# A chunked recurrence with the two heads of a pair on partition halves, transposed G and H, and the inverse applied inside the step

## The chip, the cores and the metric

One core of a Trainium2 chip runs the program; the others are idle. Its engines are TensorE (PE; its weight loads are listed apart as PEld), VectorE (DVE), ScalarE (ACT), GpSimd (POOL) and the sync engine SP, which only starts DMAs. The metric is the device time of one execution in microseconds (us); less is better.

## The reference

Two parts. First a linear recurrence on a 40 by 40 state, for 4 batches x 8 heads and 768 time steps; then a two-layer network on its outputs, 3072 rows of 320.

```python
for t in range(S):                       # S = 768, D = 40, float32
    y[:, :, t] = einsum('bhd,bhde->bhe', r_t, state)
    Sa = einsum('bhde,bhe->bhd', state, a_t)
    state = state * w_t[..., None, :] - einsum('bhd,bhe->bhde', Sa, b_t) \
            + einsum('bhd,bhe->bhde', v_t, k_t)
x = y.transpose(0, 2, 1, 3).reshape(3072, 320)
h = x @ w_in                             # 320 x 2048
out = (h * tanh(softplus(h))) @ w_out    # 2048 x 320
```

## The kernel before

**Chunks.** Time is cut into 12 chunks (`nch`) of 64 steps (`C`). Inside a chunk the recurrence becomes matrix products. With w's running products P and their inverses E folded into a and into b and k, the vectors u that the state is corrected by obey a triangular system: u = -(1 - G)^-1 (a S + H v), where G holds the products of a with b and H those of a with k, both strictly triangular in time. The outputs and the next state are then products of r, b, k, v, u and the old state S.

**Indices.** The 32 batch-head pairs are split as 2 x 2 x 8: `be` and `al` are one bit each and `s` runs over 8. Before, the partition halves of the inputs hold `al` (0 to 39 and 64 to 103), and `be` is a loop.

**Preparation of a chunk**, `pre_a(c, be)`, twice a chunk. SP loads w, a, b and k. VectorE reduces, scans forward to P (which is also stored for later, `pD`) and backward to E, multiplies a by P (L152) and b, k by E (L170). ScalarE spreads a block-diagonally into `ad` (L155). For each s one matmul of the full array gives G, H and the transposed a at once (L186, 128x168 out); ScalarE and VectorE copy the pieces into `gp`, the 32-blocks of G, and `ha`, which holds H under a mask and a (L188 to L193). Transposes give `bkn`, time on partitions (L202). Small matmuls turn w's products into `RW` (L166).

**The inverse of two chunks**, `pre_inv(n)` and `post_inv`. VectorE transposes 32-blocks (L209), solves 128 triangular 32-systems by 30 rounds of a multiply and an add (L214, L216), and transposes back (L218, L220). Two rounds of 32-square matmuls (L232, L241) give the lower left block of the 64-inverse, ScalarE lays it out block-diagonally in `bdT` (L249 to L251), and one matmul for each s (L258) multiplies the inverse into `ha`: `KT`, copied by L260.

**The step of a chunk**, `step(c)`, for two groups `g` of 8 pairs each, in the order of `SORD`. `step_a`: VS holds v and the state; 16 matmuls of VS with KT give u transposed at once (L286), which L288 writes into UVT beside v. `step_b`: UVT times r (L320), masked by VectorE into UVQ (L322). `step_u`: u itself by a transpose and a matmul with the identity for each s (L294, L296). `step_d`: the state transposed (L310). `step_c`: outputs and state update (L340, L345), then L348 to L352. `step_loads` starts the next chunk's loads from GpSimd's queue, and L376 stores the chunk's output.

**The network**, class `Mlp`. Weights arrive as 64-bit floats and are converted piece by piece (`load_f32`, `split`: L465 to L501), each split in two float32r parts. `early` loads a quarter of w_in, `first` the rest once the preparation's pools are free (`pctx`), `second` (at the last pair of chunks) the first `NO1` = 3 of 8 pieces of w_out, `third` the others when the recurrence's pools are free. `mlp1` (L591) and `mlp2` (L611 to L613) are TensorE work on 256 rows at a time, mlp2 running `LAG` = 3 quarters behind.

**Order.** A planner places every instruction on its engine's queue, in program order unless `tc.high_priority(offset)` moves a block forward (or back, if negative). The program order is preparation and inverse for pair 0, preparation for pair 1, then for each pair n the letters of `ORDER`: `0` and `1` are its two steps, `i` the inverse of pair n+1, `a` the preparation of pair n+2, `A` the call of `first`. The table `OFF` holds the offsets by block. Queues run in order; a waiting instruction holds up all that is behind it on its engine.

Of the kernel before, what the change touches and what calls it, by code (L numbers as in the profile page):

```python
# [7 lines left out]
F32 = mybir.dt.float32  # L8
F32R = mybir.dt.float32r
AF = mybir.ActivationFunctionType  # L10
ALU = mybir.AluOpType
# [4 lines left out]
NHA = 8  # L16
# [3 lines left out]
NKT = 2  # L20
# [10 lines left out]
NAD = 2  # L31
# [16 lines left out]
def layouts(inp, S=768):  # L48
    nch = S // C

    def v(x):
        return x[:, :, :S].reshape(4, 2, 2, 2, nch, C, 40)

    r, k, vv, w, a, b = (v(inp[n]) for n in 'rkvwab')
    o = {}
    wt = w.transpose(4, 2, 1, 6, 3, 0, 5).reshape(nch, 2, 2, 40, 8, C)
    wa = np.zeros(wt.shape[:4] + (1040,), np.float32)
    wa[..., :520].reshape(wt.shape[:4] + (8, 65))[..., 1:] = wt
    wa[..., 528:] = a.transpose(4, 2, 1, 6, 3, 0, 5).reshape(nch, 2, 2, 40, 512)
    o['wa'] = wa  # L60
    bt, kt = (x.transpose(4, 2, 1, 6, 3, 0, 5).reshape(nch, 2, 2, 40, 8, 1, C) for x in (b, k))
    bk = np.concatenate([bt, kt], -2)
    bk[:, 1] = np.concatenate([kt, bt], -2)[:, 1]
    o['bk'] = bk.reshape(nch, 2, 2, 40, 8, 128)
    o['rD'] = np.ascontiguousarray(r.transpose(4, 1, 6, 2, 3, 0, 5)).reshape(nch, 2, 40, 16, C)
    o['vD'] = np.ascontiguousarray(vv.transpose(4, 1, 6, 3, 0, 2, 5)).reshape(nch, 2, 40, 8, 128)
    o['vN'] = np.ascontiguousarray(vv.transpose(4, 2, 5, 3, 0, 1, 6)).reshape(nch, 2, C, 16, 40)
    p = np.arange(128)
    cst = np.zeros((128, 328), np.float32)
    cst[:, :128] = np.eye(128)  # L70
    cst[:, 128:192] = (p[:, None] % 64) < np.arange(64)
    cst[:, 192:256] = np.arange(64) < (p[:, None] // 64) * 32 + p[:, None] % 32
    cst[:, 256:296] = (p[:, None] % 64) == np.arange(40)
    cst[:, 296:328] = np.arange(32) < p[:, None] % 32
    o['cst'] = cst
    return o


def attention(ctx, tc, I, yD, pD, nch, M):
# [11 lines left out]
    ci = pool("ci", 1, ictx)  # L91
# [4 lines left out]
    cst = cs.tile([128, 328], F32, name="cst")  # L96
    ident = cst[:, 0:128]
    maskQ = cst[:, 128:192]
    maskH = cst[:, 192:256]
    maskG = cst[:, 296:328]  # L100
    wab = [cp.tile([128, 1040], F32, name=f"wa{i}") for i in range(NWA)]
    bkb = [cp.tile([128, 8, 168], F32, name=f"bk{i}") for i in range(NWA)]
    adb = [cp.tile([128, 8, 2, 2, 32], F32, name=f"ad{i}") for i in range(NAD)] * (2 // NAD)
    d1 = cp.tile([128, 584], F32, name="d1")
    bdT = [ci.tile([128, 8, 2, 64], F32, name=f"bdT{i}") for i in range(2)]
    z = cs.tile([128, 1], F32, name="z")
    V.memset(z, 0.0)
    for w, b in zip(wab, bkb):
        V.memset(w, 1.0)
        G.memset(b, 0.0)  # L110
    for t in [d1] + [x.rearrange("p s k a t -> p (s k a t)") for x in adb[:NAD]]:
        A.copy(t, z.broadcast_to(t.shape))
    for t in bdT:
        G.memset(t, 0.0)
    VS = [cs.tile([128, 2, 344], F32, name=f"VS{be}") for be in range(2)]
    UVT = cs.tile([128, 8, 256], F32, name="UVT")
    UVQ = [cs.tile([128, 16, 104], F32, name=f"UVQ{be}") for be in range(2)]
    bdr = [cs.tile([128, 2, 8, 2, 64], F32, name=f"bdr{i}") for i in range(NBR)] * (2 // NBR)
    ST = [cs.tile([128, 8, 64], F32, name=f"ST{g}") for g in range(2)]
    for t in VS + [UVT] + bdr[:NBR] + ST:  # L120
        G.memset(t, 0.0)

    RW, W2, HA, BKN, GP, KT = {}, {}, {}, {}, {}, {}
    LQ, SQ, OQ, PQ = (dict(S=SP, G=G, A=A)[x] for x in QS)

    def pre_a(c, be):
        n = 2 * c + be
        wa, bk, ad = wab[n % NWA], bkb[n % NWA], adb[n % 2]
        for al in range(2):
            q = slice(al * 64, al * 64 + 40)  # L130
            LQ.dma_start(out=wa[q], in_=I['wa'][c, be, al])
        for al in range(2):
            q = slice(al * 64, al * 64 + 40)
            LQ.dma_start(out=bk[q, :, 0:128], in_=I['bk'][c, be, al])
        if (c, be) == (0, 0):
            LQ.dma_start(out=cst, in_=I['cst'])
            for t in bkb:
                A.copy(t[:, :, 128:168], cst[:, 256:296].unsqueeze(1).broadcast_to([128, 8, 40]))
        wz, a = wa[:, 0:521], wa[:, 528:1040]
        P = pw.tile([128, 520], F32, name="P", bufs=NP)  # L140
        E = wa[:, 520:1040]
        w2 = pw.tile([128, 2, 8], F32, name="w2", bufs=4)
# [8 lines left out]
        a3 = a.rearrange("p (s t) -> p s t", t=64)  # L151
        V.tensor_tensor(out=a3, in0=a3, in1=P3[:, :, 0:64], op=ALU.mult)  # L152
        for al in range(2):
            q = slice(al * 64, al * 64 + 64)
            A.copy(ad[q, :, :, al], a[q].rearrange("p (s k t) -> p s k t", k=2, t=32))  # L155
# [3 lines left out]
        W2[be] = w2  # L159
        if be == 1:  # L160

            RW[c] = wk.tile([128, 2, 16], F32, name="rw", bufs=4)
            pt = ps_g.tile([128, 2, 16], F32, name="pa")
            for b2 in range(2):
                for al in range(2):
                    PE.matmul(pt[b2 * 64:b2 * 64 + 64, al], ident[:, al * 64:al * 64 + 64], W2[b2].rearrange("p a b -> p (a b)"),  # L166
                              start=(al == 0), stop=True, skip_group_check=True)
            A.copy(RW[c], pt)
        bk4 = bk[:, :, 0:128].rearrange("p s (x t) -> p s x t", x=2)
        V.tensor_tensor(out=bk4, in0=bk4, in1=E3[:, :, 0:64].unsqueeze(2).broadcast_to([128, 8, 2, 64]), op=ALU.mult)  # L170
        for al in range(2):
            PQ.dma_start(out=pD[c, be, :, al], in_=P[al * 64:al * 64 + 40])

        if c % 2 == 0 and be == 0:
            GP[c // 2] = iw.tile([128, 32, 2, 32], F32, name="GP", bufs=NGP)
        gp = GP[c // 2]
        u0 = (c % 2) * 16 + be * 8
        ha = iw.tile([128, 8, 104], F32, name="HA", bufs=NHA)
        HA[c, be] = ha
        oa, oh = (0, 40) if be == 0 else (64, 0)  # L180
        og, ok = (0, 64) if be == 0 else (64, 0)
        for s0 in (0, 3, 6):
            m = min(3, 8 - s0)
            pt = ps_g.tile([128, 3, 168], F32, name="pa")
            for j in range(m):
                PE.matmul(pt[:, j], ad[:, s0 + j].rearrange("p k a t -> p (k a t)"), bk[:, s0 + j], start=(j == 0), stop=True,  # L186
                          skip_group_check=True)
            A.mul(gp[0:64, u0 + s0:u0 + s0 + m, 1], pt[0:64, 0:m, og:og + 32], -1.0)  # L188
            A.mul(gp[64:128, u0 + s0:u0 + s0 + m].rearrange("p u k i -> p u (k i)"), pt[64:128, 0:m, og:og + 64], -1.0)
            A.copy(ha[:, s0:s0 + m, oa:oa + 40], pt[:, 0:m, 128:168])  # L190
            V.tensor_tensor(out=ha[:, s0:s0 + m, oh:oh + 64], in0=pt[:, 0:m, ok:ok + 64],
                            in1=maskH.unsqueeze(1).broadcast_to([128, m, 64]), op=ALU.mult)
        V.tensor_tensor(out=gp[:, u0:u0 + 8, 1], in0=gp[:, u0:u0 + 8, 1], in1=maskG.unsqueeze(1).broadcast_to([128, 8, 32]),  # L193
                        op=ALU.mult)

        bkn = wk.tile([128, 664], F32, name="bkn", bufs=NBKN)
        BKN[c, be] = bkn
        G.memset(bkn[:, 640:664], 0.0)
        for s0 in (0, 4):
            pt = ps_g.tile([128, 4, 2, 64], F32, name="pa")  # L200
            for j in range(4):
                PE.transpose(pt[:, j].rearrange("p a b -> p (a b)"), bk[:, s0 + j, 0:128], ident)  # L202
            A.copy(bkn[:, s0 * 80:s0 * 80 + 320].rearrange("p (s a e) -> p s a e", a=2, e=40), pt[:, :, :, 0:40])

    def pre_inv(n):
# [3 lines left out]
        V.transpose(X.rearrange("p t j -> p j t"), gp[:, :, 1].rearrange("p u j -> p j u"))  # L209
# [7 lines left out]
        TT = iw.tile([128, 32, 32], F32, name="TT", bufs=NTT)  # L217
        V.transpose(TT.rearrange("p u t -> p t u"), X)  # L218
        T1 = gp[0:64, :, 0]
        V.transpose(T1, TT[0:64])  # L220
        return TT, T1

    def post_inv(n, TT, T1):
        gp = GP[n]
        for h in range(2):
            with at(tc, 'T%d' % h):
                px = ps_a.tile([64, 16, 32], F32, name="pa")
                for j in range(16):
                    u = h * 16 + j
                    for al in range(2):  # L230
                        q = slice(64 + al * 32, 96 + al * 32)
                        PE.matmul(px[al * 32:al * 32 + 32, j], gp[q, u, 0], TT[q, u], start=(j == 0), stop=True,  # L232
                                  skip_group_check=True)
                X = iw.tile([64, 16, 32], F32, name="X2", bufs=NX2)
                A.copy(X, px)
# [430 lines left out]
```

## Time and profile before

| | |
|---|---|
| time of the runs | 859.57 us median of 3 (859.17 to 859.66) |
| the profiled execution | 858.42 us, of which the span of instructions is 856.6 us |
| busy: PE, PEld, DVE, ACT, POOL | 769.2, 695.8, 466.2, 429.8, 123.5 us |
| granted TensorE clock, mean | 0.95 |
| last chunk's output stored | from 510 us |

The profile page gives busy time of each engine and, in rows of 40 digits, the busy tenths of each slice of 21.4 us. "By stage" is a table of busy time in chosen stretches. A timeline row gives start, length, engine, source line, operation, tiles written and read, shape and count. A group's row gives count, busy time, mean length in ns, and the idle time of the engine before its instructions with what ended most of it. An f32 matmul appears as two records.

### The profile page before, as it was taken

The page shows a single profiled execution, that of the slowest core. Times are in us where ns is not written, and L with a number is a line of the kernel's source. Part 1 is how long each engine was busy: PE and PEld are TensorE (multiplying, and loading weights), DVE is VectorE, ACT ScalarE, POOL GpSimd, SP SyncE. Part 2 cuts the span into 40 slices and gives each one's busy share as a digit, 9 for nine tenths or more (in the row PEclk, how much of TensorE's full clock was granted, in tenths as well). Part 3 has the DMA queues.
Part 4 walks back from the last instruction along what each step waited for, and adds up shares of the span by engine and source line. Part 5 has one row for each costly group of instructions (what it writes and reads, how often), then busy time and mean ns, then how long its engine had stood idle before and what let it go on. Part 6 is the DMA issues. An engine that isn't in the chain of part 4 may idle for free.

```text
span 856.6 us, 19033 instructions
## 1 busy us (share of the span) xinstructions
PE 769.2 (90%) x7904; PEld 695.8 (81%) x7904; DVE 466.2 (54%) x975; ACT 429.8 (50%) x937; POOL 123.5 (14%) x206
## 2 busy tenths in 40 slices
PE   2545899899999999998798989999999999999998
PEld 2434777777778777876776889999999999999998
DVE  6789869758758856878663728422221222222110
ACT  4533647674564686557557626433333333333331
POOL 8100022233123213321212200000000000000000
PEclk9855699999979999999899999999999999999999
DMA  5622224443232334423425746201211121100000
GB/s 165 156 70 62 84 56 90 97 115 92 68 103 80 96 86 110 102 64 101 117 81 130 187 97 184 60 18 36 53 39 30 38 54 34 34 20 17 16 1 31
DMA packets 59750, 65.87 MB, mean 77 GB/s; under 512 B 25920, under 2 KB 49472, under 8 KB 59664
## 3 DMA queue, kind: packets, MB, share of 16 engines
q1 hardware_dynamic: 49296, 40.94, 17.2%
q0 software_dynamic: 10368, 23.72, 11.7%
q8 instruction: 62, 1.02, 0.5%
q14 instruction: 24, 0.20, 0.1%
HBM read 52.72 MB, written 11.86 MB: 75 GB/s over the span
## 4 chain that ended last, share of the span: by engine, by line
PE 59%; ACT 9%; DVE 3%; DMA 3%; issue 1%; SPq 0%; DVEq 0%; ACTq 0%
PE ph L591 19%; PE po L611 6%; PE po L612 6%; PE po L613 6%; PE pq L320 3%; PE pa L258 3%; PE pu L296 3%; PE pq L340 2%; PE pa L186 2%; PE pu L294 2%; PE pu L286 2%; PE pq L345 2%; DMA cv_d<-in_wo 2%; PE pu L310 1%; PE pa L202 1%
## 5 line engine op out<-in xcount | busy, mean ns | idle before, releaser
L591 PE MATMUL ph<-xh,w_ih 128*128 128x256 f32 x576 | 148.8, 284 | 0.0
L593 ACT ACTIVATE g<-ph 128x512 f32<-128x512 f32 x96 | 57.1, 597 | 179.0 <-PE ph L591 178.8
L597 DVE TENSOR_TENSOR gl<-g,gh 128x1024 fp32r<-128x1024 f32 x48 | 58.6, 1225 | 160.1 <-ACT gh L596 159.8
L186 PE MATMUL pa<-bk,ad 128*128 128x168 f32 x384 | 86.0, 374 | 46.5 <-DVE bk L170 16.7
L591 PE MATMUL ph<-xh,w_il 128*128 128x256 f32 x576 | 124.0, 283 | 0.0
L611 PE MATMUL po<-w_oh,gh 128*128 128x320 f32 x384 | 118.1, 310 | 1.5 <-ACT w_oh L500 1.5
L612 PE MATMUL po<-w_ol,gh 128*128 128x320 f32 x384 | 118.7, 309 | 0.0
L613 PE MATMUL po<-w_oh,gl 128*128 128x320 f32 x384 | 118.4, 309 | 0.0
L186 PEld LDWEIGHTS pa<-bk,ad 128*128 128x128 f32 x384 | 70.4, 232 | 52.9 <-issue 25.7
L591 PEld LDWEIGHTS ph<-xh,w_ih 128*128 128x128 f32 x576 | 109.5, 190 | 0.2 <-issue 0.2
L591 PE MATMUL ph<-xl,w_ih 128*128 128x256 f32 x384 | 100.6, 284 | 0.0
L591 PEld LDWEIGHTS ph<-xh,w_il 128*128 128x128 f32 x576 | 96.5, 191 | 0.2 <-issue 0.2
L611 PEld LDWEIGHTS po<-w_oh,gh 128*128 128x128 f32 x384 | 71.9, 188 | 2.2 <-ACT w_oh L500 2.2
L591 PEld LDWEIGHTS ph<-xl,w_ih 128*128 128x128 f32 x384 | 73.2, 191 | 0.1
L612 PEld LDWEIGHTS po<-w_ol,gh 128*128 128x128 f32 x384 | 72.2, 188 | 0.1
L613 PEld LDWEIGHTS po<-w_oh,gl 128*128 128x128 f32 x384 | 72.2, 188 | 0.0
L258 PE MATMUL pa<-bdT,HA 128*104 128x128 f32 x384 | 54.1, 294 | 10.4 <-ACT bdT L251 8.2
L216 DVE TENSOR_TENSOR XL<-XL,tmp 128x30 f32<-128x30 f32 (+9 forms) x180 | 59.0, 328 | 2.6
L214 DVE TENSOR_TENSOR tmp<-XL 128x30 f32<-128x30 f32 (+9 forms) x180 | 58.4, 324 | 2.5
L258 PEld LDWEIGHTS pa<-bdT,HA 128*104 128x104 f32 x384 | 47.5, 182 | 14.8 <-ACT bdT L251 9.5
L320 PE MATMUL pq<-bdr,UVT 128*128 128x128 f32 x384 | 51.1, 284 | 2.8 <-DVE UVQ L322 2.3
L596 ACT CAST gh<-g 128x1024 fp32r<-128x1024 f32 x48 | 50.1, 1047 | 1.1
(92 smaller groups left out, 1310.9 us busy)
## 6 DMA issues: line engine op xcount, KB each, us to landing
wa<-in_wa SPq DMA_DIRECT2D x48, 162.5 KB
bk<-in_bk SPq DMA_DIRECT2D x48, 160.0 KB
cv_d<-in_wi SPq DMA_DIRECT2D x12, 512.0 KB
cv_d<-in_wo SPq DMA_DIRECT2D x8, 640.0 KB
pD<-P POOLq DMA_DIRECT2D x48, 81.2 KB, 2.6
VS<-in_vN POOLq DMA_DIRECT2D x24, 160.0 KB, 3.1
UVT<-in_vD POOLq DMA_DIRECT2D x24, 160.0 KB, 3.8
bdr<-in_rD POOLq DMA_DIRECT2D x24, 160.0 KB, 4.9
```

The costliest lines, as they stand in the source:

```text
L186: PE.matmul(pt[:, j], ad[:, s0 + j].rearrange("p k a t -> p (k a t)"), bk[:, s0 + j], start=(j == 0), stop=True, skip_group_check=True)
L214: V.tensor_tensor(out=tv, in0=X[:, i + 1:32, i:i + 1].broadcast_to([128, 31 - i, i]), in1=X[:, i:i + 1, 0:i].broadcast_to([128, 31 - i, i] ...
L216: V.tensor_tensor(out=X[:, i + 1:32, 0:i], in0=X[:, i + 1:32, 0:i], in1=tv, op=ALU.add)
L258: PE.matmul(pk[:, j], ha[:, s0 + j], bd[:, s0 + j].rearrange("p a t -> p (a t)"), start=(j == 0), stop=True, skip_group_check=True)
L320: PE.matmul(pq[:, s], UVT[:, g * 4 + s, be * 128:be * 128 + 128], br[:, be, g * 4 + s].rearrange("p a t -> p (a t)"), start=(s == 0), stop ...
L591: PE.matmul(o, w, x, start=(j == 0 and n == 0), stop=(n == 7), skip_group_check=True)
L593: A.activation(g[:, f0:f0 + 2], ph, AF.Mish)
L596: A.copy(gh, g)
L597: V.tensor_tensor(out=gl, in0=g, in1=gh.bitcast(F32), op=ALU.subtract)
L611: PE.matmul(po[k], gh[:, j, t], oh, start=(f == 0), stop=False, skip_group_check=True)
L612: PE.matmul(po[k], gh[:, j, t], ol, start=False, stop=False, skip_group_check=True)
L613: PE.matmul(po[k], gl[:, j, t], oh, start=False, stop=(f == 15), skip_group_check=True)
```

## The change

The partition halves now hold `be`, and `al` is the loop (`pre_a(c, al)`). The a vectors are loaded straight into a tile `HT`, one for a chunk and four in all, and multiplied there by P, in one instruction for each half. G and H come out transposed, from 16 matmuls that use 64 rows of the array each, for the two halves in two PSUM banks; H goes into the other half of HT under one mask. `ad`, `HA`, `bdT`, `KT` and the matmuls of RW are gone. The inverse stays in a tile `TF`, its lower right block moved by two GpSimd copies and two memsets.

In the step, `step_a` computes a S + H v with HT as weights and L288's successor writes the negative, `W`; `step_u` multiplies W with the inverse, once for u transposed (`pt`, into UVT) and once for u (`pn`, into UVQ), 32 matmuls of 64 by 64 for a group. `step_b` takes 16 matmuls on 64 rows in place of 8 on 128, with r from a new tile `rT`. The order of a step has u ahead of b. `OFF` keeps three entries, and the steps of a pair stand ahead of the next inverse and preparation. `NO1` is 0, and the network's input pool `mpx` is made in `second`.

```diff
-NHA = 8
+NHT = 4
+NTF = 2
...
-ORDER = '0aiA1'
-
-OFF = {'I': 80, 'T1': 80, 'P00': -40, 'P10': 80, 'P11': 40, 'b0': 15, 'c0': 600, 'u0': -15, 'u1': 250, 'd0': 250,
-       'd1': 150, 'W': 600, 'V': 400, 'E': 150, 'I0': 600, 'I1': -15, 'I2': 15, 'I3': 150, 'I4': 80, 'p4': 15,
-       'I5': -150, 'J5': 600, 's0': 150, 's2': -15, 's3': 80, 's4': 250, 's6': -15, 's7': -40, 's8': 150, 's10': -150}
-SORD = 'a0 b0 u0 d0 a1 b1 u1 d1 c0 c1'
+ORDER = '01iaA'
+
+OFF = {'W': 600, 'V': 400, 'E': 150}
+SORD = 'a0 u0 b0 d0 a1 u1 b1 d1 c0 c1'
...
+        for be in range(2):
+            LQ.dma_start(out=wz[be * 64:be * 64 + 40], in_=I['w'][c, al, be])
+        for be in range(2):
+            LQ.dma_start(out=ht[be * 64:be * 64 + 40, al, :, be], in_=I['a'][c, al, be])
+        for be in range(2):
+            LQ.dma_start(out=bk[be * 64:be * 64 + 40], in_=I['bk'][c, al, be])
...
-        V.tensor_tensor(out=a3, in0=a3, in1=P3[:, :, 0:64], op=ALU.mult)
-        for al in range(2):
-            q = slice(al * 64, al * 64 + 64)
-            A.copy(ad[q, :, :, al], a[q].rearrange("p (s k t) -> p s k t", k=2, t=32))
...
+        for be in range(2):
+            a = ht[hb[be], al, :, be]
+            V.tensor_tensor(out=a, in0=a, in1=P3[hb[be], :, 0:64], op=ALU.mult)
...
+        pt = [ps_g.tile([128, 8, 64], F32, name="pa") for _ in range(2)]
+        for s in range(8):
+            for be in range(2):
+                PE.matmul(pt[be][:, s], bk[hb[be], s], ht[hb[be], al, s, be], start=(s == 0), stop=True, skip_group_check=True)
+        for be in range(2):
+
+            q0, q1 = slice(be * 64, be * 64 + 32), slice(be * 64 + 32, be * 64 + 64)
+            A.mul(gp[q0], pt[be][q0].rearrange("p s (k t) -> p s k t", k=2)[:, :, ::-1], -1.0)
+            A.mul(gp[q1, :, 1], pt[be][q1, :, 32:64], -1.0)
+            V.tensor_tensor(out=ht[hb[1 - be], al, :, be], in0=pt[be][hb[1 - be]],
+                            in1=mask[hb[1 - be]].unsqueeze(1).broadcast_to([64, 8, 64]), op=ALU.mult)
...
+        V.transpose(tf[:, :, 0:32].rearrange("p u t -> p t u"), X)
+        V.transpose(gp[:, :, 1], tf[:, :, 0:32])
+        for be in range(2):
+            q1 = slice(be * 64 + 32, be * 64 + 64)
+            G.tensor_copy(tf[q1, :, 32:64], tf[q1, :, 0:32])
+            G.memset(tf[q1, :, 0:32], 0.0)
...
+        pu = ps_u.tile([128, 8, 40], F32, name="pu")
+        for u in range(8):
+            for be in range(2):
+                PE.matmul(pu[hb[be], u], HT[c % NHT][:, u % 2, g * 4 + u // 2, be], VS[be][:, g, u * 40:u * 40 + 40],
+                          start=(u == 0), stop=True, skip_group_check=True)
+        A.mul(W[g][:, 0:320].rearrange("p (u d) -> p u d", d=40), pu, -1.0)
 
     def step_u(c, g):
...
+        for u in range(8):
+            t = u0 + u % 2 * 8 + u // 2
+            for be in range(2):
+                PE.matmul(pt[hb[1 - be], u], W[g][hb[be], u * 40:u * 40 + 64], tf[hb[be], t], start=(u == 0), stop=True,
                           skip_group_check=True)
+            if not last:
+                for be in range(2):
+                    PE.matmul(pn[hb[be], u], tf[hb[be], t], W[g][hb[be], u * 40:u * 40 + 40], start=(u == 0), stop=True,
+                              skip_group_check=True)
+        A.copy(UVT[:, g * 16 + 1:g * 16 + 17:2], pt)
+        if not last:
             for be in range(2):
...
+                A.copy(UVQ[be][hb[be], g * 8:g * 8 + 8, 64:104], pn[hb[be]])
...
+        pq = [ps_q.tile([128, 8, 64], F32, name="pq") for _ in range(2)]
+        for u in range(8):
+            for be in range(2):
+                t = 2 * (g * 8 + u) + 1 - be
+                PE.matmul(pq[be][:, u], UVT[hb[1 - be], t:t + 2].rearrange("p a t -> p (a t)"), r[hb[1 - be], g * 8 + u],
+                          start=(u == 0), stop=True, skip_group_check=True)
...
-NO1 = 3
+NO1 = 0
...
-        if NQ1 == 4:
-            self.mpx = self.pool("mpx", 2)
...
-            self.mpx = self.pool("mpx", 2)
+        self.mpx = self.pool("mpx", 2)
```

More of the change, by code (lines that the diff above doesn't have):

```diff
@@ L19 @@
 NWA = 2
-NKT = 2
 NXL = 1
@@ L94, in attention @@
     pw = pool("pw", 2, pctx, "right")
-    cst = cs.tile([128, 328], F32, name="cst")
+    cst = cs.tile([128, 224], F32, name="cst")
     ident = cst[:, 0:128]
[L98 to L103, printed above, removed]
+    mask = cst[:, 128:192]
@@ L182, in pre_a @@
[L182 to L192, printed above, removed]
@@ L288, in step_a @@
[L288 to L297 removed]
+                A.copy(VS[be][srow[be], g].rearrange("p (s d) -> p s d", d=40), st[srow[be], :, 0:40])
```

229 lines of the change are left out of this document (85 added, 144 removed).

## The prediction

> **What bounds the kernel now.** I read the page's slices first, then the busy time by stage, then the TensorE timeline of one stretch for the real spacing of matmuls, then the groups by shape.
>
> ```profile
> PE 769.2 (90%) x7904; PEld 695.8 (81%) x7904; DVE 466.2 (54%) x975; ACT 429.8 (50%) x937; POOL 123.5 (14%) x206
> PE   2545899899999999998798989999999999999998
> DVE  6789869758758856878663728422221222222110
> ```
>
> ```profile
> 0.00:110.00 110.00, 58.68 (x396) 49.67 (x397) 92.34 (x207) 52.40 (x140) 27.38 (x50) 0.74 0.39 107
> 110.00:390.00 280.00, 261.69 (x3440) 213.54 (x3439) 211.09 (x524) 179.42 (x471) 72.90 (x124) 0.98 0.36 90
> 390.00:510.00 120.00, 107.17 (x1489) 91.84 (x1489) 70.92 (x149) 71.05 (x146) 22.26 (x31) 0.94 0.48 120
> 510.00:550.00 40.00, 38.47 (x288) 37.73 (x288) 26.23 (x33) 22.81 (x32) 1.00 (x2) 1.00 0.42 127
> 550.00:857.00 307.00, 303.24 (x2299) 302.98 (x2298) 65.62 (x64) 104.08 (x150) 0.00 (x0) 1.00 0.12 31
> ```
>
> The second block's columns are stretch, length, then busy time of PE, PEld, DVE, ACT, POOL with counts, granted clock, DMA share, GB/s. Five stages stand out. To 110 us the preparation and first inverse run, with VectorE (DVE) busy 92.3 of 110. From 110 to 390 eight chunks of the recurrence run beside the remaining preparation: 280/8 = 35 us a chunk, TensorE (PE) busy 93%, DVE 75%, ScalarE 64%. From 390 to 510 the last four chunks run beside the loading of w_in. Then w_out is loaded, and from 550 TensorE alone sets the pace; the change touches nothing there. So only the first 550 us can move, and 110 to 390 is a TensorE stage with VectorE second.
>
> **The change, part by part.** Busy time of pipelined matmuls overlaps, so I cost them by start-to-start spacing. Columns: start, length, engine, line, tiles, shape, count.
>
> ```profile
> 247.38 1.98 PE L186 MATMUL pa<-bk,ad 128*128 128x168 f32 x12
> 249.28 0.81 PE L241 MATMUL pa<-X,GP 32*32 32x32 f32 x38
> ...
> 255.97 1.99 PE L258 MATMUL pa<-bdT,HA 128*104 128x128 f32 x16
> ...
> 258.78 0.88 PE L232 MATMUL pa<-TT,GP 32*32 32x32 f32 x42
> 259.59 2.05 PE L320 MATMUL pq<-bdr,UVT 128*128 128x128 f32 x16
> 261.47 0.27 PE L294 MATMUL pu<-cst,UVT 128*64 128x128 f32 x1
> ...
> 262.11 0.43 PE L296 MATMUL pu<-cst,UVT 128*64 128x128 f32 x2
> 262.48 0.30 PE L294 MATMUL pu<-cst,UVT 128*64 128x128 f32 x1
> 262.70 0.43 PE L296 MATMUL pu<-cst,UVT 128*64 128x128 f32 x2
> ...
> 264.56 1.15 PE L286 MATMUL pu<-KT,VS 104*64 104x64 f32 x32
> 265.64 0.37 PE L232 MATMUL pa<-TT,GP 32*32 32x32 f32 x10
> ```
>
> An f32 matmul stands as two records. Per record: L186 (G) (249.28-247.38)/12 = 0.158 us; L320 (step_b) (261.47-259.59)/16 = 0.117; L258 (K times inverse) about (1.99-0.29)/15 = 0.113, taking off one record's length; L286 (step_a) (265.64-264.56)/32 = 0.034, far below 0.113, because its two column halves of the array run side by side. L232 works on 32-row squares that differ in rows and columns: (259.59-258.78)/42 = 0.019, also two side by side. The transposes of step_u are the odd case: one L294 and two L296 take 262.70-262.11 = 0.59 us, three records at 0.20, each switch between the two forms costing a gap.
>
> Records per chunk, removed: G 32 x 0.158 = 5.1; K times inverse 32 x 0.113 = 3.6; step_u 8 x 0.59 = 4.7; step_b 32 x 0.117 = 3.7. Sum 17.1 us. Added: G as 64 records (64 rows, 128 weight columns, 64 moving columns), step_b as 64 of the same form, step_u as 128 records of 64 by 64. Step_a keeps 64 records (128 rows, 64 columns), step_c, step_d, the bkn transposes and the block matmuls of the inverse keep count and form, so nothing.
>
> ```profile
> L320 PEld LDWEIGHTS pq<-bdr,UVT 128*128 128x128 f32 x384 | 46.6, 194 | 4.4 <-DVE UVQ L322 2.5 <-issue 0.7 <-ACT UVT L288 0.4
> L340 PEld LDWEIGHTS pq<-UVQ,bkn 128*64 128x64 f32 x768 | 38.8, 140 | 5.5 <-ACT yev L349 1.7 <-issue 0.9 <-DVE XL L216 0.2
> ```
>
> The weight load grows by (194-140)/64 = 0.84 ns a column, so 128 columns occupy about 0.108 us. The new G and step_b move only 64 columns, but their weights are still 128 columns wide, so a row half cannot run faster than about 0.112 us a record. Whether the halves at partitions 0 and 64 run side by side, no row shows for halves that share all columns. Side by side: 32 x 0.112 = 3.6 us each for G and step_b. One behind the other: 7.2 each. For step_u, pairs at L286's 0.034 give 128 x 0.034 = 4.4; four squares at once, 2.2; nothing side by side, 8.7. I take pairs everywhere, since the nearest rows (L286, L232) both show two: 3.6 + 3.6 + 4.4 = 11.6, so -5.5 us a chunk, between -7.7 (four squares) and +6.0 (none).
>
> The Trainium skill (TensorE: Matmul & The Clock Gate, "LDWEIGHTS (loading the stationary operand)") says that load time goes by weight columns and not by contraction rows, P/1.2 ns. That speaks against the change, and the 0.84 ns a column above agrees; it makes the halves load-bound, as counted. The same page (Part 3, "Measured speedup vs the span model") gives 3.07 times for four row tiles at once; by it the halves overlap and the sum is the -5.5. No run here shows it for rows alone.
>
> VectorE and ScalarE, by these groups (columns: count, busy us, mean ns, idle before):
>
> ```profile
> L216 DVE TENSOR_TENSOR XL<-XL,tmp 128x30 f32<-128x30 f32 (+9 forms) x180 | 59.0, 328 | 2.6
> L214 DVE TENSOR_TENSOR tmp<-XL 128x30 f32<-128x30 f32 (+9 forms) x180 | 58.4, 324 | 2.5
> L322 DVE TENSOR_TENSOR UVQ<-pq,cst 128x512 f32<-128x512 f32 x48 | 32.8, 687 | 24.6 <-PE pq L320 24.4
> L191 DVE TENSOR_TENSOR HA<-pa,cst 128x192 f32<-128x192 f32 x48 | 17.0, 355 | 31.7 <-ACT HA L190 30.6 <-PE pa L186 1.0
> L152 DVE TENSOR_TENSOR wa<-wa,P 128x512 f32<-128x512 f32 x24 | 16.4, 685 | 0.0
> L218 DVE STREAM_TRANSPOSE TT<-XL 128x1024 f32<-128x1024 f32 x6 | 11.7, 1950 | 0.1
> L220 DVE STREAM_TRANSPOSE GP<-TT 64x1024 f32<-64x1024 f32 x6 | 7.3, 1224 | 0.0
> L191 DVE TENSOR_TENSOR HA<-pa,cst 128x128 f32<-128x128 f32 x24 | 6.8, 283 | 1.0 <-ACT HA L190 0.9
> L155 ACT COPY ad<-wa 64x512 f32<-64x512 f32 x48 | 29.6, 617 | 17.1 <-DVE wa L152 6.5 <-PE pa L186 5.0 <-issue 3.8
> L260 ACT COPY KT<-pa 104x512 f32<-104x512 f32 x48 | 27.4, 586 | 11.2 <-PE pa L258 10.0 <-PE pu L286 0.5
> ```
>
> VectorE gains work. The product of a becomes two instructions of 64 partitions, each still 512 elements long: 2 x 0.685 more a chunk, +1.37. The mask on H becomes four of 512 (2.75) for four of 192 and two of 128 (1.99): +0.76. The second transpose back covers 128 partitions: 1.95 for 1.22, per two chunks, +0.36. Sum +2.5 us a chunk; from 211.1/8 = 26.4 it rises to 28.9. ScalarE loses at least L155 and L260, (29.6+27.4)/12 = 4.8 us a chunk and the copies into bdT, and gains two copies for the inverse at some 0.6 each; it stays third. GpSimd gets two rT loads a chunk and, in each inverse, two copies and two memsets which stand in the chain between the last transpose and the block matmuls; its queue also holds the step's loads, which wait for step_a, step_b and step_c. 72.9 busy of 280 leaves room; I price it at nothing, and at up to 10 us an inverse where a load ahead of it waits. SP gets six loads for four in each pre_a; a now lands in HT, so the load waits for step_a four chunks earlier, with the bk load behind it. BKN's eight buffers already tie pre_a to the same chunk, so nothing. In step_c the RW matmuls (8 records a chunk) go.
>
> Stage 110 to 390: TensorE from 35 to 35-5.5 = 29.5 a chunk, VectorE at 28.9. Neither leaves cover for the other. At the 93% that the bound engine reached here, VectorE gives 31.1; with two engines near full I take 32.5, bounds 31.1 and 35: 8 x 32.5 = 260, -20 (bounds -31 and 0). The step's chain gets longer: U now needs W out of PSUM, a second round of matmuls and a copy, some 2.2 + 0.3 + 0.6 us a group ahead of step_b; it is covered by preparation and inverse. Stage 0 to 110: VectorE +2.1 in each chunk prepared against fewer ScalarE copies between; no change.
>
> **The tail.** These rows are the inverse of the last pair (first and last transpose), the outputs of chunks 9, 10, 11, and the first and last late piece of w_out:
>
> ```profile
> 386.09 2.13 DVE L209 STREAM_TRANSPOSE XL<-GP 128x1024 f32<-128x1024 f32 x1
> 439.40 1.23 DVE L220 STREAM_TRANSPOSE GP<-TT 64x1024 f32<-64x1024 f32 x1
> ```
>
> ```profile
> 460.63 1.09 POOL L376 DMA_DIRECT2D yD<-yev  x2
> 490.57 1.09 POOL L376 DMA_DIRECT2D yD<-yev  x2
> 510.26 1.00 POOL L376 DMA_DIRECT2D yD<-yev  x2 [18.60 <-ACT yev L349]
> ```
>
> ```profile
> 524.23 0.74 ACT L500 ACTIVATE w_oh<-cv_w 128x640 fp32r<-128x640 f32 x1
> 540.28 0.74 ACT L500 ACTIVATE w_oh<-cv_w 128x640 fp32r<-128x640 f32 x1
> ```
>
> The inverse is (58.4+59.0)/6 + 2.13 + 2 x 1.95 = 25.6 us of VectorE but took 54, held back by its offset of -150; that offset goes. In the new order it stands behind steps 8 and 9 (some 11 us of VectorE) and the w_in conversions (about 11): 47 us, then 4 for the blocks, then two steps of 20 (the last step, 490.57 to 510.26): 91 for the 120 now. I take -30, bounds -40 and 0. Against it NO1=0 moves three pieces of w_out behind the recurrence's end. Late pieces come every (540.28-524.23)/4 = 4.0 us, so the last comes 12 later, with first-layer matmuls for part of that: +8, bounds 0 and +12.
>
> Sum against the profiled execution: its span 856.6 plus 1.8 around it is 858.4, 0.1% under the median 859.57. 858.4 - 20 - 30 + 8 = 816.
>
> **The rivals.** A, slower: row halves do not overlap, so G and step_b take 7.2 each. Then a chunk costs TensorE 18.8 for 17.1, +1.7: 8 x 1.7 = 14 in the main stage; in the tail four chunks lose 3.5-0.3 each and two save K times inverse, 7.2: +6; no gain elsewhere, and w_out +8: 886. For it: no row-only pair in the trace. Against: L232's squares in different rows run side by side. It decides when a pair's spacing exceeds 0.112 by half, where the 5.5 a chunk falls to 2. B, nothing gained in the main stage: without offsets steps wait for the inverse. A pair then costs 25.6 + 5 + 2 x (20+3) = 77 for 70, +28 over four pairs, and only the tail's order helps: 858 + 28 - 30 + 8 = 864, or 850 where half is covered. For it: the inverse is one long VectorE chain and GpSimd's copies stand in it. Against: with preparation in program order behind it, a waiting step costs only its own queue. C, better than forecast: VectorE at 31.1 and tail at -40, w_out hidden: 787.
>
> **How the numbers follow.** Forecast 0.58, C 0.08, B 0.19, A 0.15. The likeliest alone spans 790 to 842. The range 785 to 868 takes in C and most of B and leaves out A and what is below C. What can be told from no change is 0.2%, under 2 us. Faster: forecast, C and a quarter of B, 0.71; same 0.04; slower 0.25.
>
> **What would show it.** Right: L258's group gone; G and step_b in pairs starting a few ns apart with about 0.11 between pairs; step_u 128 records a chunk without gaps of 0.2; VectorE above 85% busy while preparation runs; last output near 460. Wrong: halves in single file; VectorE idle on GpSimd; w_out gaps over 20 us.

## The result, and the profile after

The changed kernel takes 983.27 us (median of 4, 980.51 to 984.09) against 859.62 for the kernel before (859.17 to 861.58): ratio 1.143, 95% interval 1.140 to 1.146. That is 124 us slower, where 816 was predicted. The profiled execution took 982.52 us, of which the span is 980.4. Runs over 1.5% above the fastest of the same kernel, with a lower granted clock, are left out of what follows: one each of e10, f5 and f6, and one of the kernel before.

The page of the changed kernel: busy time, and the rows of tenths, each slice now 24.5 us.

```profile
PE 812.2 (83%) x9400; PEld 766.2 (78%) x9400; DVE 492.4 (50%) x975; ACT 337.0 (34%) x621; POOL 166.4 (17%) x257
PE   3744598898589848985888379999999999999998
DVE  7889959458646754585166722285222222222110
PEclk9999999558655775587565758799999999999999
```

By stage, the same columns as before (stretch, length, busy time of PE, PEld, DVE, ACT, POOL with counts, granted clock, DMA share, GB/s):

```profile
110.00:200.00 90.00, 79.61 (x1410) 73.09 (x1404) 60.43 (x137) 35.99 (x77) 24.93 (x40) 0.84 0.35 78
200.00:300.00 100.00, 79.28 (x1164) 71.23 (x1163) 62.60 (x146) 31.89 (x69) 25.19 (x40) 0.64 0.38 74
300.00:400.00 100.00, 77.29 (x1120) 69.85 (x1118) 58.99 (x129) 30.65 (x67) 25.18 (x40) 0.64 0.38 74
400.00:500.00 100.00, 81.15 (x1170) 73.04 (x1168) 54.80 (x130) 32.80 (x71) 23.22 (x37) 0.64 0.34 67
```

The last outputs stored:

```profile
553.10 1.08 POOL L349 DMA_DIRECT2D yD<-yev  x2
602.59 1.08 POOL L349 DMA_DIRECT2D yD<-yev  x2
631.29 1.00 POOL L349 DMA_DIRECT2D yD<-yev  x2 [27.62 <-ACT yev L322]
```

The recurrence ends at 631 for 510 before, +121. What follows takes 980.4 - 631.3 = 349 us against 856.6 - 510.3 = 346. So nearly the whole loss lies in the recurrence. There TensorE is still busy 80% of the time and VectorE only 60%. The one number that changed out of all proportion is the granted clock: 0.64 where the kernel before had 0.98 (110 to 390 us) and 0.94 (390 to 510).

What the clock does to the new matmuls is seen in the TensorE timeline: the first and last records of a group of step_u (64 records of L263 and L267), one group of step_b (L293, 32 records) in a stretch at full clock, and one at half clock, with the clock of the two L293 stretches below.

```profile
145.00 0.27 PE L263 MATMUL pu<-TF,W 64*64 64x64 f32 x2
...
145.93 0.22 PE L263 MATMUL pu<-TF,W 64*64 64x64 f32 x2
...
150.89 2.00 PE L293 MATMUL pq<-rT,UVT 64*128 64x64 f32 x32
...
206.42 3.68 PE L293 MATMUL pq<-rT,UVT 64*128 64x64 f32 x32 [0.69 <-ACT UVT L269]
...
255.41 0.88 PE L313 MATMUL pq<-UVQ,bkn 128*64 128x104 f32 x16
256.12 0.61 PE L318 MATMUL pq<-bdr,smd 128*64 128x128 f32 x8
```

```profile
150.90:152.90 2.00, 2.00 (x39) 1.93 (x40) 2.00 (x5) 0.00 (x0) 0.00 (x0) 1.00 0.81 210
206.40:210.10 3.70, 3.68 (x33) 3.57 (x34) 0.26 (x1) 0.70 (x2) 0.00 (x0) 0.50 0.45 85
```

At full clock 32 records take 2.00 us: taking off one record's 0.28, 1.72/15.5 = 0.111 us for two, so the two row halves do run side by side and cost what was predicted (0.112). At half clock the same group takes 3.68, 0.21 for two (starts of its pairs in the trace). One trap lies here: a group at 120 us also takes 3.7, and the profile gives that stretch a clock of 1.00, but this trace has no clock event before 140 us. I first read that group as halves standing in single file; some of the expectations below still do.

Why TensorE waits, and what a wait does. The inverse's transposes on VectorE (the last row opens the inverse two pairs later), the stretch of TensorE around its end, and the clock there:

```profile
195.21 1.93 DVE L186 STREAM_TRANSPOSE XL<-GP 128x1024 f32<-128x1024 f32 x1
267.75 1.90 DVE L197 STREAM_TRANSPOSE TF<-XL 128x1024 f32<-128x1024 f32 x1
269.69 1.25 DVE L198 STREAM_TRANSPOSE GP<-TF 128x1024 f32<-128x1024 f32 x1
...
394.18 1.93 DVE L186 STREAM_TRANSPOSE XL<-GP 128x1024 f32<-128x1024 f32 x1
```

```profile
257.25 1.13 PE L250 MATMUL pu<-VS,HT 128*64 128x40 f32 x32
270.99 1.92 PE L213 MATMUL pa<-GP 32*32 32x32 f32 x64 [12.61 <-DVE GP L198]
```

```profile
259.00:270.00 11.00, 0.00 (x0) 0.00 (x0) 7.68 (x20) 0.86 (x2) 4.59 (x8) 0.54 0.98 127
```

```profile
DVE HT L169 <- ACT GP L168: 71.5, 18, 11.8
ACT GP L167 <- PE pa L163: 58.3, 16, 6.4
PE pa L213 <- DVE GP L198: 48.8, 4, 15.4
```

The inverse, 25.6 us of VectorE work by the prediction's count, now takes 75.7 (195.2 to 270.9), where the kernel before needed 44 to 55. In these 75.7 us VectorE is busy 51.0, half of it with other work in its queue, and idle 24.7; some 19 of the idle time end at a product of TensorE, or at ScalarE's copy of one. Over the window of the last three rows, 110 to 620 us (total, times, longest), the masks on H wait 71.5 us for ScalarE's copies of G, and these copies wait 58.3 us for TensorE. TensorE in turn waits for the inverse four times, 48.8 us in all, and behind each of these waits the clock is at half.

### The profile page after: what moved, and what is told of

Same layout as the page of the kernel before. It is cut to its first block, busy times and chain, and to the rows that moved or that the text cites. A ratio compares the mean times of both kernels' runs of the same rounds, so it can differ in the third digit from the quotient of the medians.

```text
span 980.4 us, 21838 instructions
## 1 busy us (share of the span) xinstructions
PE 812.2 (83%) x9400; PEld 766.2 (78%) x9400; DVE 492.4 (50%) x975; ACT 337.0 (34%) x621; POOL 166.4 (17%) x257
## 4 chain that ended last, share of the span: by engine, by line
PE 70%; DVE 11%; DMA 11%; ACT 4%; issue 3%; SPq 1%; POOL 0%; DVEq 0%; ACTq 0%
PE ph L562 18%; PE pa L163 9%; PE pq L293 8%; PE po L582 6%; PE po L583 6%; PE po L584 6%; PE pq L313 4%; DMA cv_d<-in_wi 4%; PE pa L179 4%; DMA bk<-in_bk 3%; PE pa L223 2%; PE pq L318 2%; PE pa L213 2%; PE pu L267 2%; PE pu L250 1%
## 5 line engine op out<-in xcount | busy, mean ns | idle before, releaser
L163 PE MATMUL pa<-HT,bk 64*128 64x64 f32 x768 | 106.1, 395 | 31.6 <-DVE bk L152 22.0
L163 PEld LDWEIGHTS pa<-HT,bk 64*128 64x128 f32 x768 | 97.8, 299 | 41.4 <-issue 28.8
L293 PE MATMUL pq<-rT,UVT 64*128 64x64 f32 x768 | 88.1, 384 | 16.5 <-DVE UVQ L296 10.7
L293 PEld LDWEIGHTS pq<-rT,UVT 64*128 64x128 f32 x768 | 83.1, 290 | 22.7 <-DVE UVQ L296 9.5
L169 DVE TENSOR_TENSOR HT<-pa,cst 64x512 f32<-64x512 f32 x48 | 33.1, 689 | 78.0 <-ACT GP L168 77.3
L213 PE MATMUL pa<-GP 32*32 32x32 f32 x768 | 22.4, 233 | 59.0 <-DVE GP L198 58.1
L213 PEld LDWEIGHTS pa<-GP 32*32 32x32 f32 x768 | 20.8, 147 | 60.8 <-DVE GP L198 59.0
L313 PE MATMUL pq<-UVQ,bkn 128*64 128x104 f32 (+1 forms) x768 | 61.8, 310 | 7.1 <-ACT yev L322 4.9
```

The costliest lines, as they stand in the source:

```text
L163: PE.matmul(pt[be][:, s], bk[hb[be], s], ht[hb[be], al, s, be], start=(s == 0), stop=True, skip_group_check=True)
L169: V.tensor_tensor(out=ht[hb[1 - be], al, :, be], in0=pt[be][hb[1 - be]], in1=mask[hb[1 - be]].unsqueeze(1).broadcast_to([64, 8, 64]), op=A ...
L213: PE.matmul(px[q1, j], gp[q0, h * 16 + j, 0], gp[q0, h * 16 + j, 1], start=(j == 0), stop=True, skip_group_check=True)
L293: PE.matmul(pq[be][:, u], UVT[hb[1 - be], t:t + 2].rearrange("p a t -> p (a t)"), r[hb[1 - be], g * 8 + u], start=(u == 0), stop=True, ski ...
L313: PE.matmul(py[hb[be], 2 * j + al, 0:n], BKN[c, al][:, (2 * s + be) * 40:(2 * s + be) * 40 + 64], UVQ[be][:, 2 * s + al, 0:n], start=(j == ...
```

## The experiments

Each has the median and, where its comparison allows, the ratio to the kernel before on the same chip with its 95% interval. The medians of that kernel on those chips lie between 854 and 859 us.

**e1_squares.** G and step_b in squares, each wide half cut in two column halves:

```diff
-PE.matmul(pq[be][:, u], UVT[hb[1 - be], t:t + 2]..., r[hb[1 - be], g * 8 + u], ...)
+for be, h in ((0, 0), (1, 1), (0, 1), (1, 0)):
+    PE.matmul(pq[be][hb[h], u], UVT[hb[1 - be], t + h], r[hb[1 - be], g * 8 + u], ...)
```

> The changed kernel with each matmul of G and of step_b, 64 rows by 128 weight columns, written as two of 64 by 64 into the same places, so that four squares of the array are in use as in step_u. Theory W (wide halves): two row halves with the same 128 columns load their weights one behind the other, 0.107 us a record, and fill so little of the array that the clock falls. Then squares run at step_u's 0.015 us a record, G and step_b cost 3.7 us a chunk instead of 13.7, the granted clock of the main stage goes from 0.64 to 0.85 or more, and the time from 982 to 850-890. Theory O (order): the late inverse, which lost its early priority, sets the pace; TensorE waits as before, and the time stays at 940 or more.

Measured: 879.73 us, ratio 1.028 (1.006 to 1.050), clock 0.80 and 0.74 from 200 to 400 us, short of the 0.85 expected. The wide halves carry about 103 of the 124 us. The timeline of this kernel, with the clock of that stretch:

```profile
120.01 1.99 PE L294 MATMUL pq<-rT,UVT 64*64 64x64 f32 x64 [0.69 <-ACT UVT L270]
121.78 2.02 PE L163 MATMUL pa<-HT,bk 64*64 64x64 f32 x30
```

```profile
120.00:121.80 1.80, 1.79 (x66) 1.79 (x67) 1.40 (x3) 0.70 (x2) 0.00 (x0) 0.50 0.77 126
```

From first start to last end the same products take 1.99 us at half clock, for 3.68 as wide halves; to the start of the next group it is 1.77, 121.78 - 120.01.

**e2_old_offsets**, the changed kernel with the whole old table of priorities, and **e3_before_new_order**, the kernel before with the new order and the short table.

```diff
-OFF = {'W': 600, 'V': 400, 'E': 150}
+OFF = {'I': 80, 'T1': 80, 'P00': -40, ...}   # e2; e3 is the reverse, with ORDER '01iaA'
```

> The changed kernel with the old table OFF of priorities back in place; the order of the blocks stays the new one. Theory O: the inverse is early again, TensorE no longer waits for its last transpose (49 us in the main stage), and the time falls from 982 to 880-920. Theory W: G and step_b still take 0.107 us a record and the clock stays under 0.75 in the main stage; time 940-980.

> The kernel before with the new ORDER and the short table OFF; nothing else changed. Theory O: it loses most of what the changed kernel lost, 930 us or more, with TensorE waiting for the inverse. Theory W: its matmuls fill the array, the clock of 110 to 390 us stays above 0.9, and it lies between 860 and 890.

Measured: e2 1004.05 us, ratio 1.173 (1.151 to 1.196), slower still and outside both expectations, so the old offsets do not repair the new structure. e3 867.14, ratio 1.013 (0.994 to 1.033): the order costs the old structure about 11 us at most likely, which its interval doesn't tell from nothing.

**e4_full_rows.** step_b over all 128 rows, r beside zeros in two tiles.

```diff
-UVT[hb[1 - be], t:t + 2]..., r[hb[1 - be], g * 8 + u]
+UVT[:, t:t + 2]..., rT[1 - be][:, g * 8 + u]
```

> The changed kernel with step_b's matmuls over all 128 rows: r stands in two tiles whose other half is zero, the weights are the same 128 columns over both halves, 64 records a chunk as now. Their spacing stays at 0.107 to 0.112 us, only the filled area doubles. If the gate goes by the filled area (rows by columns by time), the granted clock of the main stage rises from 0.64 to 0.75 or more and the time falls by 20 to 60 us; if it goes by TensorE being busy or idle at all, the clock stays within 0.05 and the time within 15 us of 982.

Measured: 985.21 us, ratio 1.151 (1.122 to 1.181), clock 0.67, 0.75 and 0.73 in the stages from 200 to 500 us, for 0.64. The expectation rested on the misread group: full rows take 0.113 us a record at full clock in this trace, as much as two wide halves. So the edit doubles step_b's time and fills no more of the array for each microsecond, and it doesn't tell the clock from the loads.

**e5_squares_a, e8_wide_a.** a loaded into a tile of its own and multiplied into HT, with squares and with wide halves.

```diff
-LQ.dma_start(out=ht[be * 64:be * 64 + 40, al, :, be], in_=I['a'][c, al, be])
+LQ.dma_start(out=ab[n % NWA][be * 64:be * 64 + 40], in_=I['a'][c, al, be])
```

> The 64 by 64 squares of e1, and a is loaded into a small tile of its own, two buffers, from which VectorE multiplies it into HT; the load no longer waits for HT's slot, and bk's load no longer stands behind it on SP. Theory D: what was left in e1 (880 against 856 before) is VectorE standing in its queue before a product whose load came late (HT and bk loads of 4.5 to 7.7 us in the chain), with the inverse's last transposes behind it; time 845-865. Theory O (the inverse's place in the order alone): no more than 8 us are gained, 872 or more.

> The changed kernel, wide halves kept, with a in a tile of its own as in e5. Theory W holds the wide halves for the main cost: 960-985, since TensorE stays the slow part. Theory D alone: 900-940.

Measured: e5 883.58 us, ratio 1.035 (1.019 to 1.052), no gain over e1. e8 952.30, ratio 1.116 (1.096 to 1.136), 31 below the changed kernel (23 by the ratios) and between its two theories. The load into HT cost something only beside wide halves.

**e6_inv_first, e7_inv_early.** e5 with the next inverse ahead of the steps, and with priorities for it.

```diff
-ORDER = '01iaA'
+ORDER = 'i01aA'                  # e6
+OFF = {..., 'I': 80, 'I0': 600, 'T1': 80}   # e7
```

> e5 with ORDER 'i01aA': the next inverse stands ahead of both steps in program order. Theory O: the inverse ends before the steps of its pair do, TensorE's wait for the last transpose (51 us in e1's main stage) goes, time 820-850. Theory D: e5 has already taken most of it; within 10 us of e5.

> e5 with the program order as it is and three of the old offsets back, I 80, I0 600, T1 80, which move the inverse forward. Theory O: 825-855, near e6. Theory D: within 10 us of e5.

Measured: 882.45 us, ratio 1.034 (1.019 to 1.049), and 895.43, ratio 1.049 (1.034 to 1.065). TensorE still waits 41 and 54 us for the inverse. No place in the order that I tried gave the rest back.

**e11_g_squares.** Only G in squares.

> The changed kernel with G and H alone in squares of 64 by 64; step_b keeps its 64 rows by 128 columns. Both squares together had brought 983 to 880 us. Theory E (each wide product costs its records alone, 64 a chunk at 0.107 for each of the two): half of the gain, 925 to 940 us. Rival S (step_b stands in the chain of the step that the next inverse and chunk wait for, G beside it): G alone brings less than a third, 950 to 970, with the granted clock still near 0.64 from 200 to 500 us. Rival C (the clock recovers with either of them): clock above 0.72, 890 to 915.

Measured: 937.77 us, ratio 1.095 (1.086 to 1.105): 45 of the 103 us. That leaves about half for step_b, by difference; step_b alone in squares was not run. The clock stayed at 0.66, 0.63 and 0.61 in the stages from 200 to 500, so one of the two wide products is enough to keep it low, and this gain is that of shorter products at a low clock: by the two groups above some 3.68 - 1.99 = 1.7 us a group, two groups a chunk, 41 over twelve chunks if all ran at half clock, an estimate.

**e12_half_inverse, f4_wide_half_inverse.** The first 15 of the inverse's 30 rounds left out, with squares (from e5) and with wide halves.

```diff
-for i in range(1, 31):
+for i in range(16, 31):
```

> The version with squares and a in a tile of its own (883.6 us), with only the second 15 of the 30 rounds of the inverse: the first 15 rounds are left out, half of the elements, 12 us of VectorE for each pair. Theory V (what is left over the kernel before is VectorE's time and the inverse's chain on it): 12 us for each of five inverses, 820 to 835 us, and the steps' waits for the inverse halve. Rival T (TensorE at a clock of 0.75 sets the pace): 865 to 884, TensorE busier, waits for it elsewhere.

> The changed kernel, wide halves kept, with only the second 15 of the 30 rounds of the inverse (the first 15 left out, 12 us of VectorE a pair). Theory K with the wait for the inverse as what lets the clock fall: shorter idle stretches, clock above 0.72, and more than 12 us a pair gained: 880 to 910 us. Theory L: 12 us for each of five inverses at the most, 920 to 945, clock as before. If the clock falls by the wide halves alone: 940 to 970.

Measured: e12 840.57 us, ratio 0.982 (0.974 to 0.990), 43 under e5, more than its rival allows and less than its theory said; f4 930.97, ratio 1.084 (1.078 to 1.091), 52 under the changed kernel, as its theory L said. The wait rows of e5, then of e12, between 110 and 520 us:

```profile
PE pa L216 <- DVE GP L201: 43.2, 4, 15.2
```

```profile
PE pa L226 <- POOL TF L204: 21.0, 5, 6.8
```

With squares the wait for the inverse goes, and GpSimd's copies of TF, hidden till then, take 21 us of it (25 in f4). In f4 the clock stays at 0.70, 0.66 and 0.62 in the stages from 200 to 500: shorter waits alone don't bring it back where the halves are wide.

**f2_fill_bg, f3_fill_all, f1_fill_bg_one, f6_wide_a_fill.** Wide halves kept, with matmuls that only fill the array: k = 3 ahead of each PSUM tile of G and step_b (f2), also ahead of step_u and the inverse's blocks (f3), k = 1 (f1), and k = 1 on e8 (f6).

```diff
+for _ in range(k):
+    PE.matmul(o[:, 0:224], ident, cst, start=True, stop=True, ...)
```

> The changed kernel with work that only fills the array: ahead of G and of step_b, three matmuls with the identity over 224 columns into each PSUM tile, which the real ones then overwrite; 24 a chunk, 0.19 us of streaming each at full clock, 4.5 us a chunk. Theory K (the loss is the granted clock: at full clock two wide halves do run in 0.112 us a pair, at half clock in 0.214; back to back they stream for a quarter of the time, and the clock stays low): clock from 200 to 500 us 0.75 or more instead of 0.64, time 900 to 965 us in spite of 54 us of added work. Theory L (the wide halves cost their weight loads, and the clock decides nothing): the filler comes on top, 1020 to 1060 us.

> The same, with such fillers also ahead of step_u (three for each group) and of the inverse's block matmuls (six for each of four PSUM tiles a pair), where TensorE has just waited: some 8 us a chunk at full clock. Theory K: clock 0.85 or more in the stage, time below f2's by 10 to 40 us, 880 to 950. Theory L: 1050 to 1100 us.

> The changed kernel with one filler matmul of 224 columns ahead of each PSUM tile of G and step_b, eight a chunk for the 24 of f2: 1.5 us a chunk, 18 us in all. Theory K by streamed area: a group of 32 records takes 1.8 us at full clock and streams for 0.43 of it; with 0.37 of filler 0.80 of 2.2 us, 0.37 of the array, at the edge of what kept the clock full in the traces (0.35 to 0.4): clock 0.70 to 0.85 from 200 to 500 us, 920 to 960 us. If the edge lies lower, the clock goes to 0.9 as in f2 and 36 us less filler shows: 890 to 915. If the fillers work only by keeping the queue busy, 975 to 1000.

> The same single filler on the version with wide halves and a in its own tile (952.3 us). The a tile was worth 30 us on the changed kernel and nothing with squares. If that gain was the clock's too, it shrinks beside a filler: within 10 us of f1. If it is a matter of the load queue, it adds up: 20 to 35 us below f1.

Measured: f2 930.09 us, ratio 1.083 (1.077 to 1.089); f3 956.63, 1.114 (1.108 to 1.120); f1 921.65, 1.076 (1.069 to 1.084). The fillers' groups in f2 and one stretch of them, its stages, its last output, and its wait for the inverse (110 to 520 us):

```profile
L95 PE MATMUL pa<-cst 128*128 128x224 f32 x288 | 83.3, 442 | 3.0 <-DMA cst<-in_cst 2.9
L95 PE MATMUL pq<-cst 128*128 128x224 f32 x288 | 71.1, 383 | 3.0 <-DVE UVQ L304 2.9
```

```profile
207.73 2.54 PE L95 MATMUL pq<-cst 128*128 128x224 f32 x12
```

```profile
200.00:300.00 100.00, 92.14 (x1533) 80.06 (x1530) 76.24 (x176) 38.35 (x84) 28.48 (x45) 0.95 0.43 89
300.00:400.00 100.00, 92.28 (x1540) 80.58 (x1538) 79.04 (x178) 38.18 (x83) 32.76 (x51) 0.95 0.47 93
```

```profile
574.86 1.00 POOL L357 DMA_DIRECT2D yD<-yev  x2 [25.02 <-ACT yev L330]
```

```profile
PE pa L219 <- DVE GP L204: 18.3, 4, 10.4
```

The expectations count a filler as one record of 0.19 us ((2.54-0.38)/11 = 0.196 here); it is two, so f2 added 576 records, some 109 us, twice what was said, and f1 36. This is the direct test of the clock: 109 us of useless work make the kernel 53 us faster. The clock in these stages goes from 0.64 to 0.95, VectorE from 61% to 78%, the recurrence ends 56 us earlier, the inverse that starts at 205 us takes 47 instead of 75.7, and the wait for it falls from 48.8 to 18.3 us. f1 gains 62 us with a third of the work and a clock between (0.88, 0.74, 0.74); f3 drives the clock to 0.98 and TensorE to 93 to 97% busy, where the filler itself becomes the load; its time lies outside both expectations. f6 took 915.02 us in one run, 7 under f1; one run leaves open whether a's own tile adds to the filler.

**f5_squares_fill.** e5 with fillers ahead of step_u (2) and the inverse's blocks (4).

> The version with squares and a in its own tile (883.6 us), with two fillers ahead of step_u for each group and four ahead of each PSUM tile of the inverse's blocks, some 3.5 us a chunk at full clock. Theory K: clock in the stage above 0.85 from 0.75, 855 to 878 us. Rival V (VectorE and the inverse set what is left over the kernel before; the clock is only their shadow): the clock rises, the time does not fall: 880 to 900 us.

Measured: 878.85 us in one run, against e5's 883.58 (881.53 to 885.64), with the clock up from 0.78 to 0.88 and from 0.72 to 0.85:

```profile
200.00:300.00 100.00, 82.87 (x1976) 71.31 (x1976) 85.69 (x206) 43.45 (x96) 33.87 (x53) 0.88 0.48 100
300.00:400.00 100.00, 82.65 (x1966) 70.36 (x1966) 72.47 (x157) 43.55 (x94) 36.72 (x59) 0.85 0.47 97
```

By the same count its fillers are some 54 us of TensorE. They cost nothing and bring at most some 5 us, between its two expectations: with squares TensorE's clock isn't what keeps the kernel 23 us above the one before. VectorE, 86% busy in the first of these stages, and the inverse's chain on it are the nearer cause, and e12 speaks for it; one run doesn't show it.

**e10_before_u_halves.** The kernel before, with the transpose in step_u written as the matmul that its other half already is.

```diff
-PE.transpose(pt[0:64, s]..., UVT[:, g * 4 + s, 0:64], ident)
-PE.matmul(pt[64:128, s]..., UVT[:, g * 4 + s, 192:256], ident, ...)
+for be in range(2):
+    PE.matmul(pt[be * 64:be * 64 + 64, s]..., UVT[:, g * 4 + s, be * 192:be * 192 + 64], ident, ...)
```

> The kernel before, with the transpose of u (step_u, L294) written as the same matmul with the identity that its other half (L296) already is, so that both halves of the columns have one form. Theory P (the stage from 110 to 390 us is set by TensorE, and the gaps of 0.2 us at each switch of form are TensorE time): eight times a chunk the 0.59 us of four records falls to about 0.23, so 2.9 us a chunk, 23 over eight chunks and up to 10 in the tail: 825 to 838 us. Rival V (VectorE, 75% busy, and the inverse take over at once): half of it or less, 842 to 852. Rival N (the gaps lie beside waits): 855 to 860.

Measured: 842.19 us (836.55 to 845.47), ratio 0.982 (0.972 to 0.993): faster than both kernels. Its timeline, and its last output:

```profile
256.31 1.09 PE L295 MATMUL pu<-cst,UVT 128*64 128x128 f32 x16
```

```profile
494.11 1.00 POOL L375 DMA_DIRECT2D yD<-yev  x2 [15.53 <-ACT yev L348]
```

Sixteen records in 1.09 us, (1.09-0.28)/15 = 0.054 each for 0.20 before: two column halves side by side, with no switch between forms. So four records of 0.22 us replace three of 0.59 (the expectation calls these four), eight times a chunk, 36 us over twelve chunks. The recurrence ends 16 us earlier, about half of that, as its rival V had it.

## Why the prediction was wrong

**The step that failed** is the one that was not written down: every duration was taken at the clock of before (0.98 from 110 to 390 us) and kept for the changed kernel. The forecast had TensorE at 29.5 us a chunk. Divided by the granted 0.64 that is 46; the trace shows (394.18-195.21)/4 = 49.7 from one inverse to the one two pairs on. The terms that carry it are G and step_b: 32 x 0.112 = 3.6 us each as forecast, but 32 x 0.21 = 6.7 at half clock.

**Why the clock fell.** An f32 column takes 0.85 ns at full clock: L313's 16 records, two halves side by side, start 0.71 us before the next line (255.41 to 256.12), 0.089 for 104 columns. So I estimate how much of the array streams. L320 of before: 128 columns, 109 ns of 117, over 0.9 at full clock and a half at half clock. The wide halves: 64 columns, 54 ns of 112, a half at full clock but only a quarter (54 of 214) at half clock. The squares of e1 at half clock: 54 ns for each four records of 27.6, again a half.

The trace gives the clock in steps of 3.41 us. I worked out the streamed share of each step up to 640 us, taking for every record rows x columns x moving columns x 0.85 ns from its start on: of 230 steps of the changed kernel, e1 and e4 below 0.30 of the array, none was followed by full clock; of 190 above 0.40, 188 were, and of the 25 of these at half clock, 24. In seven more traces (before, f1, f2, f4, e5, e8, e11) it was 7 of 457 and 575 of 578. How long TensorE was busy doesn't tell them apart: of 119 half-clock steps of the first three kernels in which it was busy 99% or more, 29 were followed by full clock.

So a wait of 11 us (259 to 270) takes the clock away. In the trace the clock falls twelve times between 140 and 620 us: in the four waits for the inverse, and eight times beside waits of 1.0 to 4.0 us, five of them for step_b's mask (L296) and one, of 4.0 us, for GpSimd's copies of TF. Matmuls that fill half the array at half clock bring it back in a step; the wide halves at half clock stay below the line and hold it down until step_c's matmuls come. With fillers, a group of step_b at half clock streams (0.86+0.76)/2/(1.8+0.76) = 0.32 in f1 and (0.86+2.27)/2/(1.8+2.27) = 0.38 in f2, an estimate by the same column time (0.86 us of products, 0.76 or 2.27 of filler, and 1.8 us for the group without filler at full clock): one near the lower end of what the steps leave open (0.30 to 0.40), one near its upper end, as their clocks came out. That the clock is what the wide halves lose by is shown by f1 and f2, and that they hold it down by e1, with e11 for one product alone; where the line lies is read from the traces only.

The Trainium skill (TensorE: Matmul & The Clock Gate, "HAM oscillation — how this bites in real kernels") says that TensorE must have no idle gaps over some 3.4 us. The wait at 259 agrees; but the clock also fell beside shorter ones, such as 2.97 us ending at 235.72. By that rule alone a TensorE busy 80% would have recovered behind it; here the clock was at half in 206.4 to 210.1 with TensorE busy 3.68 of 3.70 us, so a busy queue isn't enough, and the measurement decides.

**The change, point by point.** The wide pair: predicted 0.112 us, measured 0.111 at full clock. Step_u: predicted pairs at 0.034 a record; 64 records start between 145.00 and 145.93, 0.015 each, four squares at once, so this term came out better. The K times inverse group is gone as said. VectorE's predicted bound never came: it fell to 60% busy. "I price it at nothing", of GpSimd's copies, nearly held in the changed kernel, with one wait of 4.0 us, because the inverse was later still: with that shortened, e12 shows 21 us of wait for them. "a now lands in HT ... so nothing" was wrong by some 23 to 31 us with wide halves (e8), and held with squares (e5).

**The tail** was to be 30 us shorter. From 510 before, the end moved to 631, and its chunks suffer the same clock (0.61 from 500 to 600), so the reordering's own worth was never seen. NO1 = 0 was given +8; the rest after the recurrence grew by 3 us, within its bounds.

**The rivals.** A had the right place and sign and the wrong mechanism: the halves do overlap. Its 886 lacked what the waits and the clock add to each other. B's mechanism, steps waiting for the inverse, is in the trace (48.8 us), and it opens the door to the half clock four times of twelve; priced at full clock it gave 864. The 23 us that e1 keeps over the kernel before look to be of B's kind: e1 still waits 51 us for the inverse, e12 takes 43 us away by shortening it, no order tried on the squares did (e6, e7), and e3 puts about 11 on the order, with an interval that includes none. How the 23 divide stays open.

## What to carry to other kernels

When matmuls are cut into smaller pieces, count beside their time how much of the array streams, at half clock too: a form that is bound by its weight load can run as fast as forecast at full clock and still hold the clock down once a wait has dropped it. Cut rows and columns together (squares, four at once) rather than rows alone, so that weights and columns halve alike. And check that a term's durations and the stage that it is moved to have the same clock.

## What the runs showed of the hardware

In these traces the clock follows the streamed share of the array rather than how busy TensorE is: below 0.30 of the array in a step of 3.41 us it was all but never full in the next, above 0.40 nearly always. Useless full-array matmuls, 9 us a chunk, raised it from 0.64 to 0.95 and more than paid for themselves; 3 us a chunk gave as much time. A load-bound pair slows with the clock as well, 0.111 to 0.21 us. A transpose among matmuls of another form cost 0.2 us a record where matmuls of one form cost 0.054. And a clock of 1.00 ahead of a trace's first clock event says nothing: at 120 us, 20 us before it, a group of 32 wide halves took 3.7 us, as at half clock.
